# An adaLN + S4D convolution + ReLU MLP kernel: the last doubling ahead of h's shift, kernel products between h's transforms, and two butterfly steps summed on TensorE

## The chip, the cores and the metric

The kernel runs as one program on one core of a Trainium2 chip. The metric is the device time of one execution in microseconds (us), as the median of three runs; smaller is better. Five engines work side by side and meet at semaphores: TensorE (PE, with its weight loads as PEld), VectorE (DVE), ScalarE (ACT), GpSimd (POOL) and SyncE (SP, which here only issues DMAs). Each of them works through its own instructions strictly in the order in which the program lists them.

## The reference

One block of a network on x of 2048 tokens by 576 channels, all in float32. `c` gives six modulation vectors, a layer norm and a long convolution along the tokens are added to x, and then a layer norm and a two-layer ReLU network of width 4608:

```
mod = (silu(c) @ w_mod).reshape(1, 6, 1, 576)      # sa, ca, ga, sb, cb, gb
h = layernorm(x) * (1 + ca) + sa
x = x + ga * conv(h)                                # below
h = layernorm(x) * (1 + cb) + sb
x = x + gb * (relu(h @ w1) @ w2)

def conv(u):                                        # one filter of 2048 taps for each channel
    dt = exp(log_dt);  A = -exp(log_A_real) + 1j * A_imag
    C = (C_real + 1j * C_imag) * dt
    P = exp(A * dt * pos)                           # 576 x 128 states x 2048 positions
    K = 2 * real(sum over states of C * P)
    return irfft(rfft(K, 4096) * rfft(u, 4096))[:2048] + u * D_skip
```

## The kernel before

**Blocks.** The tokens are cut into four blocks of 512, and the filter into four pieces of 512 taps. `Body.conv(s)` does the convolution of block s in the frequency domain, `Body.ffn` the ReLU network of the same block; the convolution of block s+1 is worked off in pieces inside the network of block s (`step`). Only block 0 has nothing to hide behind: what runs before the network of block 0 starts is called the front part here. The change touches the front part alone.

**The front part** makes the first filter piece, transforms it and block 0, multiplies, and transforms back. All of its instructions carry `Kept(...)` or `keep_in_program_order`, so the order in which the Python code emits them is the order on each engine.

- `KGen.first` makes the filter in six groups g of 96 channels. For each group DVE builds `W1` (16 powers, by four doublings in `doubling`; in the fourth, m == 8, DVE makes four products into `T0`/`T1` and POOL adds them), ACT, DVE and POOL build `W2` (32 powers), and TensorE sums `W2` times `W1` over the states into `kps` (`products`, 96 small matmuls for each of two halves u of a group). ACT copies `kps` into `ke` (`rows`), and SP stores `ke` to DRAM (`kd`) once three groups are done. `kt_0` and `kt` are the two channel halves p = 0, 1 of the piece, loaded back from `kd` in transform layout; half 1 needs group 5, the last one. `skip` adds the D_skip term to one row of `kt`.
- The hooks `"first"`, `"late"` and `"rows"` of `conv(0)` are the last group's products of half u = 0, of half u = 1, and then `save` (W1 to DRAM), the copy to `ke` and the store to `kd`.
- `Body.early` is a generator that `first` advances: statistics of x, the normalised `h`, then `h`'s shift, which is eight DVE operations (times `m_ca`, plus `m_sa`).
- A spectrum is made in two stages. `transform` does eight matmuls of 128x288 (four tiles n2 by real and imaginary part c) into `ps_f`, and ACT copies each to `Z`. Then `butterfly` combines the four tiles on DVE in two steps: `butterfly1` (sums and differences of tiles i and i+2, four operations, into `W`) and `butterfly2` (six operations, into `U` or `K`). `transform1` does the first step on TensorE instead: 16 matmuls that accumulate in pairs, the second of a pair with `fcK` or with its negative `fcKn`. Before the change half 1 of the filter takes `transform1`, half 0 takes `transform`.
- `product` multiplies K and U into `Y`, `back` is the inverse's butterfly on DVE into `V`, and `inverse` does the inverse's matmuls into `ps_i`, which DVE adds to x. For half 0 `back` does only the first step and `inverse` the second on TensorE (16 matmuls, some with `gcn`, the negatives of `gc`); for half 1 `back` does both steps and `inverse` 8 matmuls.
- `norm2` follows: statistics, scaling, transposes `ps_t`, then `xh`, `xl`, `xs`, the operands of the network. The first matmul `hps` of `ffn` ends the front part.

A float32 matmul shows in the profile as two records of PE, so eight matmuls of a transform are x16.

**Queues and buffers around it.** POOL issues the saves of the spectra (`Ud` for U, `Rd` for K of block 0); SP issues `kd`, `kt`, the modulation weights `wm_sb`, `wm_cb`, `wm_gb`, the saves of W1, W2 and the network's weights (`r`, with `L1d`/`L2d` the stores of their low halves). Spectra share six buffers (`S`), so a later tile waits until an earlier one has been read and saved. `mod_late` makes three modulation vectors on TensorE (`mps_sb`, `mps_cb`, `mps_gb`). In `ffn`, `hi1`/`hi2` (ACT) and `lo1`/`lo2` (DVE) split a weight tile into a high and a low part.

Of the kernel before, what the change touches and what calls it, by code (L numbers as in the profile page):

```python
# [49 lines left out]
class KGen:  # L50
# [274 lines left out]
    def first(self, setup, mod):  # L325
# [43 lines left out]
        def run(*gens):  # L369
            for x in gens:  # L370
                for _ in x:
                    pass
# [24 lines left out]
        for g in range(NG):  # L397
# [26 lines left out]
            else:  # L424
                run(late, double[3])
            if g + 1 == NG:
                next(early)
            if g > 0:
                rows(g - 1)
            run(*double[4:])  # L430
            if g + 1 < NG:
                save(g)
# [141 lines left out]
class Body:  # L574
# [34 lines left out]
    def early(self, kg):  # L609
# [11 lines left out]
        for i in range(4):  # L621
            yield
            st = sm.tile([P, 2, 6], F32, tag="st", bufs=8, name="st0")
            for p in range(2):
                kept(nc.vector.bn_stats(out=st[:, p], in_=x2[:, i, p * PC : (p + 1) * PC]))
            kept(nc.vector.bn_aggr(out=mv[:, i, 0:2], in_=st))
# [8 lines left out]
        for i in (0, 2, 1, 3):  # L635
            kept(nc.scalar.activation(
                h[:, i], x2[:, i], AF.Identity, scale=mv[:, i, 3:4], bias=mv[:, i, 4:5]
            ))
        yield
        self.kt0 = kg.kt0  # L640
        kept(self.skip(self.kt0, 0, nc.vector))
        for i in (0, 2, 1, 3):
            kept(nc.vector.tensor_tensor(h[:, i], h[:, i], self.m["ca"], op=ALU.mult))
            kept(nc.vector.tensor_tensor(h[:, i], h[:, i], self.m["sa"], op=ALU.add))
# [294 lines left out]
    def conv(self, s):  # L939
# [11 lines left out]
        else:  # L951
            x2, h = self.x2[0], self.h0
            self.fcKn, self.gcn = (
                self.cv.tile([P, 4, P], F32, name=n) for n in ("fcKn", "gcn")
            )
            for t, a in zip((self.fcKn, self.gcn), self.I["neg"]):
                nc.gpsimd.dma_start(out=t, in_=a)
        def kernel_tile(p):
# [13 lines left out]
        def mm_K(p, Z):  # L972
# [3 lines left out]
            src = lambda n2: ktv[:, n2 // 2, :, n2 % 2]  # L976
            if s == 0 and p == 1:
                return self.transform1(src, self.fcK, self.fcKn, Z)
            return self.transform(src, self.fcK, Z, s == 0)

        def spec_U(p, Z):
            U = self.spec(f"U_{s}_{p}")
            yield from self.butterfly(Z, U, -1)
            yield -1
            if s + 1 < NB or p == 1:
                self.save(self.Ud[s][p], U)
            Us.append(U if s == 0 or p == 0 else None)

        def spec_K(p, Z):
            R = self.load(self.Rd[s - 1][p], "R") if s > 0 else None  # L990
            K = self.spec(f"K_{s}_{p}")
            yield from (self.butterfly2 if s == 0 and p == 1 else self.butterfly)(Z, K, -1)
            yield -1
# [50 lines left out]
        def inverse(p, V, tiles=(0, 2, 1, 3)):  # L1044
            g = lambda n2, c: self.gc[:, n2, c, :]
            neg = lambda i: self.gcn[:, i, :]
            for n2 in tiles:
                ps = self.cps.tile([P, 512], F32, tag="cps", bufs=self.nps, name="ps_i")
                if s or p == 1:
                    ops = [(g(n2, c), V[:, n2, c]) for c in range(2)]  # L1050
# [16 lines left out]
        def back(p, Y):  # L1067
            V = self.spec(f"V_{s}_{p}")
            yield from self.butterfly1(Y, V) if s == 0 and p == 0 else self.butterfly(Y, V, 1)
            Vs.append(V)  # L1070
# [4 lines left out]
        if s == 0:  # L1075
            yield from mm_K(0, ZK)
            yield from mm_U(0, ZU)
            Z1 = self.spec("Z")
            yield from mm_U(1, Z1)
            for hook in ("first", "late", "rows"):  # L1080
                yield hook
            kt[1] = kernel_tile(1)
            yield "weights"
            yield "mod"
            yield "mod"
            yield "mod"
            yield "high"
            yield from spec_U(0, ZU)
            yield from spec_U(1, Z1)
            yield from spec_K(0, ZK)  # L1090
            ZK = self.spec("Z")
            yield from mm_K(1, ZK)
            self.save(self.Rd[0][0], Ks[0], Kept(self.tc, nc.gpsimd))
        else:
# [170 lines left out]
    def ffn(self, gens):  # L1265
# [166 lines left out]
        yield  # L1432
        lo1(0)
        lo2(0)
        lo1(1)
        yield
        load_r2(1)
# [200 lines left out]
```

## Time and profile before

| | |
|---|---|
| median of 3 runs | 1322.19 us (1321.43 to 1322.21) |
| the profiled execution, its own time | 1322.81 us |
| its span (first to last instruction) | 1321.0 us |
| mean granted TensorE clock | 0.946 |
| PE busy, share of the span | 1210.7 us, 92% |
| DVE busy, share of the span | 895.0 us, 68% |
| DMA, mean over the span | 262 GB/s |
| first `hps` matmul (end of the front part) | 220.30 us |

All times below are from the span's start. In a timeline a line gives start, length, engine, source line, operation, out<-in, shapes, count, and in brackets the idle time of the engine ahead of it with what ended it. Operations of a helper have the helper's line: L62 is DVE in the filter generator, L68 its POOL, L71 its matmuls, L47 any `Kept` operation, L852 the matmuls of `transform`, L891 and L893 those of `transform1`, L1059 those of `inverse`. In the chain of waits "issue" is time in which an engine waited for nothing that the profile shows.

### The profile page before, as it was taken

How to read it: one execution, taken by the hardware profiler on the slowest of the kernel's cores; microseconds unless marked ns; L12 is line 12 of the kernel's file. 1: busy time of each engine (PE TensorE's matmuls, PEld its weight loads, DVE VectorE, ACT ScalarE, POOL GpSimd, SP SyncE). 2: the span in 40 equal slices, each digit the busy share in tenths (PEclk: the TensorE clock that was granted, in tenths of full speed). 3: DMA queues.
4: the chain of work that ended last, by engine and by line, in shares of the span. 5: the costliest groups of instructions: out<-in, count | busy, mean ns of one | idle time of the engine just before them, and what ended most of it. 6: DMA issues, size and time to landing. Idle time of an engine off the chain costs nothing.

```text
span 1321.0 us, 25994 instructions
## 1 busy us (share of the span) xinstructions
PE 1210.7 (92%) x10720; PEld 959.5 (73%) x10720; DVE 895.0 (68%) x1324; ACT 494.8 (37%) x863; POOL 160.3 (12%) x256
## 2 busy tenths in 40 slices
PE   4666686999999998999999999999999999999998
PEld 2444564677767776787777887887888888888886
DVE  7889988999976999589468994557996222111112
ACT  5787523222223422622243225433323452233231
POOL 1666411011000100110011000100000000000000
PEclk9556787999899999999999999999999999999999
DMA  8757982988778977799889985868996667666662
GB/s 274 269 200 289 322 304 85 349 308 322 286 256 303 345 241 262 261 406 336 279 276 336 360 323 156 294 198 294 343 382 198 172 179 227 202 194 197 195 178 71
DMA packets 118027, 345.85 MB, mean 262 GB/s; under 512 B 17772, under 2 KB 19604, under 8 KB 107156
## 3 DMA queue, kind: packets, MB, share of 16 engines
q1 hardware_dynamic: 101332, 228.14, 51.9%
q0 software_dynamic: 16064, 114.67, 23.0%
q8 instruction: 84, 1.38, 0.4%
q10 hardware_dynamic: 512, 1.38, 0.4%
q14 instruction: 35, 0.29, 0.1%
HBM read 262.73 MB, written 81.40 MB: 261 GB/s over the span
## 4 chain that ended last, share of the span: by engine, by line
PE 75%; DVE 14%; DMA 6%; issue 4%; ACT 1%; POOL 1%; SPq 0%; ACTq 0%; DVEq 0%; POOLq 0%
PE hps L1332 31%; PE acc L1358 30%; PE ps_f L852 5%; PE kps L519 3%; PE kps L71 2%; DMA L1d<-w 2%; PE ph L71 2%; PE ps_i L1059 2%; DVE T L484 1%; DVE W1r L486 1%; DMA x<-in_x_dram 1%; DVE T L62 1%; DMA Ua<-Ud 1%; DVE W L62 1%; DVE w L1302 1%
## 5 line engine op out<-in xcount | busy, mean ns | idle before, releaser
L1332 PE MATMUL hps<-xh,w 128*128 128x512 f32 x1152 | 394.2, 403 | 0.8 <-ACT xh L47 0.8
L1358 PE MATMUL acc<-w,hh 128*128 128x512 f32 x1136 | 362.1, 401 | 4.9 <-ACT hh L1337 3.4
L1338 DVE SCALAR_TENSOR_TENSOR hl<-hps,hh 128x512 fp32r<-128x512 f32 x144 | 99.2, 689 | 306.9 <-ACT hh L1337 306.2
L1332 PEld LDWEIGHTS hps<-xh,w 128*128 128x128 f32 x1152 | 217.8, 190 | 48.3 <-ACT xh L47 1.4
L1358 PEld LDWEIGHTS acc<-w,hh 128*128 128x128 f32 x1136 | 212.5, 188 | 51.3 <-ACT hh L1337 4.3
L1332 PE MATMUL hps<-xl,w 128*128 128x512 f32 x576 | 227.4, 396 | 0.0
L1358 PE MATMUL acc<-w,hl 128*128 128x512 f32 x568 | 221.0, 402 | 1.6 <-DVE hl L1338 1.6
L1337 ACT ACTIVATE hh<-hps 128x512 fp32r<-128x512 f32 x144 | 86.0, 597 | 324.7 <-PE hps L1332 317.5
L1307 ACT ACTIVATE w<-r 128x576 fp32r<-128x576 f32 x141 | 96.7, 686 | 229.0 <-PE acc L1358 221.4
L1332 PEld LDWEIGHTS hps<-xl,w 128*128 128x128 f32 x576 | 109.1, 189 | 22.9
L1358 PEld LDWEIGHTS acc<-w,hl 128*128 128x128 f32 x568 | 106.9, 190 | 25.3 <-DVE hl L1338 3.0
L1297 ACT ACTIVATE w<-r 128x640 fp32r<-128x640 f32 x140 | 102.6, 733 | 40.6 <-DMA L1d<-w 38.1
L1332 PE MATMUL hps<-xs,w 128*128 128x512 f32 x288 | 98.3, 411 | 0.0
L71 PE MATMUL kps<-W,W 128*32 128x16 f32 x2304 | 40.3, 211 | 44.9 <-POOL W L68 28.4
L1038 DVE TENSOR_TENSOR Y<-Y,T 128x1152 f32<-128x1152 f32 x60 | 79.4, 1351 | 0.0
L71 PEld LDWEIGHTS kps<-W,W 128*32 128x32 f32 x2304 | 35.5, 145 | 58.8 <-POOL W L68 31.0
L853 ACT ACTIVATE Z<-ps_f 128x288 f32<-128x288 f32 x120 | 48.9, 409 | 71.9 <-PE ps_f L852 70.1
L519 PEld LDWEIGHTS kps<-W1r,W2r 128*32 128x32 f32 x3456 | 45.1, 113 | 37.8 <-issue 23.1
L519 PE MATMUL kps<-W1r,W2r 128*32 128x48 f32 (+2 forms) x3456 | 52.5, 201 | 14.4 <-issue 8.8
L1332 PEld LDWEIGHTS hps<-xs,w 128*128 128x128 f32 x288 | 53.5, 189 | 11.2
L1358 PE MATMUL acc<-hh,w 128*128 128x512 f32 x142 | 56.7, 399 | 0.0
L1358 PE MATMUL acc<-hl,w 128*128 128x512 f32 x142 | 56.0, 394 | 0.0
(249 smaller groups left out, 1543.5 us busy)
## 6 DMA issues: line engine op xcount, KB each, us to landing
r<-in_w_dram SPq DMA_DIRECT2D x144, 320.0 KB, 5.9
r<-in_w_dram SPq DMA_DIRECT2D x144, 288.0 KB, 3.6
w<-L1d SPq DMA_DIRECT2D x108, 320.0 KB, 3.9
w<-L2d SPq DMA_DIRECT2D x108, 288.0 KB, 2.7
W2r<-W2d POOLq DMA_DIRECT2D x18, 1536.0 KB, 8.8
W2d<-W SPq DMA_DIRECT2D x12, 1536.0 KB, 8.5
Ua<-Ud POOLq DMA_DIRECT2D x15, 1152.0 KB, 9.4
W<-W1d POOLq DMA_DIRECT2D x18, 768.0 KB, 9.4
```

Source lines behind the costliest of these rows:

```text
L62: self.tc.keep_in_program_order(self.nc.vector.tensor_tensor(out, a, b, op=op))
L71: self.tc.keep_in_program_order(self.nc.tensor.matmul(*args, **kw))
L519: nc.tensor.matmul(ps[32 * dd : 32 * dd + 32, q, :], W2[:, r, ch], W1[:, r, ch], start=(r == 0), stop=(r == 1),)
L852: nc.tensor.matmul(o, fc[:, n2, c, :], src(n2), start=True, stop=True)
L853: ev = nc.scalar.activation(Z[:, n2, c], ps[:, :PC], AF.Copy)
L1038: v(y, y, T, op=op or ALU.add)
L1297: copy(g - 1)(w1[g][:, 0], r1[g], AF.Copy)
L1307: copy(g)(w[:, 0:D], r2[g], AF.Copy)
L1332: nc.tensor.matmul(ps, a, x, start=(i == 0), stop=(i == 13))
L1337: nc.scalar.activation(hh, ps, AF.Relu)
L1338: nc.vector.scalar_tensor_tensor(hl, ps, 0.0, hh, op0=ALU.max, op1=ALU.subtract)
L1358: nc.tensor.matmul(acc[i], a, x, start=(f == 0 and seen[i] == 1), stop=(f == NF - 1 and seen[i] == (3 if i < 4 else 2)),)
```

## The change

Six edits, all in the front part.

1. In `first`, the step of `early` with h's shift comes after the last group's fourth doubling instead of before it; `skip` of `kt_0` moves from that step into the one before.
2. Filter half 0 is transformed with `transform1` (16 matmuls instead of 8), so `spec_K(0)` does only `butterfly2`. `fcKn` is loaded by SP early instead of by POOL late.
3. `conv(0)` runs the last group's products of half u = 0 ahead of h's first transform, and those of half u = 1 with the copy and store of `ke` between h's two transforms. Before, all of them came after both.
4. The spectrum of the filter half comes ahead of the two of h on DVE. The saves of U and K (`Ud`, `Rd`) are issued by POOL after `skip` of `kt`.
5. The modulation vector gb is made after the transform of filter half 1 instead of before it.
6. For output half 1, `back` does only the first step (four operations into V, in another order than before), and `inverse` does the second on TensorE. `lo2(0)` and `lo1(1)` of the network's weights move to the next step of `ffn`, behind `norm2`.

```diff
@@ KGen.first
-            if g + 1 == NG:
-                next(early)
             if g > 0:
                 rows(g - 1)
             run(*double[4:])
+            if g + 1 == NG:
+                next(early)
@@ Body.early
         for i in range(4):
             yield
+            if i == 1:
+                self.fcKn = sm.tile([P, 4, P], F32, name="fcKn")
+                nc.sync.dma_start(out=self.fcKn, in_=I["neg"][0])
...
-        yield
         self.kt0 = kg.kt0
         kept(self.skip(self.kt0, 0, nc.vector))
+        yield
         for i in (0, 2, 1, 3):
             kept(nc.vector.tensor_tensor(h[:, i], h[:, i], self.m["ca"], op=ALU.mult))
@@ Body.conv
-            self.fcKn, self.gcn = (
-                self.cv.tile([P, 4, P], F32, name=n) for n in ("fcKn", "gcn")
-            )
-            for t, a in zip((self.fcKn, self.gcn), self.I["neg"]):
-                nc.gpsimd.dma_start(out=t, in_=a)
+            self.gcn = self.cv.tile([P, 4, P], F32, name="gcn")
+            nc.gpsimd.dma_start(out=self.gcn, in_=self.I["neg"][1])
@@ mm_K
-            if s == 0 and p == 1:
+            if s == 0:
                 return self.transform1(src, self.fcK, self.fcKn, Z)
-            return self.transform(src, self.fcK, Z, s == 0)
+            return self.transform(src, self.fcK, Z)
@@ spec_U
-            if s + 1 < NB or p == 1:
+            if s and (s + 1 < NB or p == 1):
                 self.save(self.Ud[s][p], U)
@@ spec_K
-            yield from (self.butterfly2 if s == 0 and p == 1 else self.butterfly)(Z, K, -1)
+            yield from (self.butterfly if s else self.butterfly2)(Z, K, -1)
@@ inverse
-                if s or p == 1:
+                if s:
                     ops = [(g(n2, c), V[:, n2, c]) for c in range(2)]
@@ back
-            yield from self.butterfly1(Y, V) if s == 0 and p == 0 else self.butterfly(Y, V, 1)
+            if s:
+                yield from self.butterfly(Y, V, 1)
+            else:
+                for i, op in ((0, ALU.add), (1, ALU.add), (0, ALU.subtract), (1, ALU.subtract)):
+                    v(V[:, 2 * i + (op == ALU.subtract)], Y[:, i], Y[:, i + 2], op=op)
+                yield -1
@@ conv, block 0
             yield from mm_K(0, ZK)
+            yield "first"
             yield from mm_U(0, ZU)
+            yield "late"
+            yield "rows"
             Z1 = self.spec("Z")
             yield from mm_U(1, Z1)
-            for hook in ("first", "late", "rows"):
-                yield hook
             kt[1] = kernel_tile(1)
             yield "weights"
             yield "mod"
             yield "mod"
-            yield "mod"
             yield "high"
+            yield from spec_K(0, ZK)
             yield from spec_U(0, ZU)
             yield from spec_U(1, Z1)
-            yield from spec_K(0, ZK)
             ZK = self.spec("Z")
             yield from mm_K(1, ZK)
-            self.save(self.Rd[0][0], Ks[0], Kept(self.tc, nc.gpsimd))
+            for dst, t in ((self.Ud[0][0], Us[0]), (self.Rd[0][0], Ks[0]), (self.Ud[0][1], Us[1])):
+                self.save(dst, t, Kept(self.tc, nc.gpsimd))
+            yield "mod"
@@ ffn
         lo1(0)
+        yield
+        lo1(1)
         lo2(0)
-        lo1(1)
-        yield
```

Where the instructions stand is shown at three places. First TensorE and VectorE around h's shift. `kps_2248` (after: `kps_2250`) holds the last group's products, `W_5` is its W1, `W_10` and `W_11` are its W2 of the halves u = 0 and 1, `fcU` is h's transform matrix, `mps_sb` the first late modulation vector. TensorE before:

```order
L71 MATMUL kps_1942<-W_4_1712,W_9_1706 32x16 x96
L852 MATMUL ps_f<-kt_1943,fcK 128x288 x8
L852 MATMUL ps_f<-h_2099,fcU 128x288 x16
L71 MATMUL kps_2248<-W_5_2048,W_10_2041 32x16 x96
L71 MATMUL kps_2248<-W_5_2048,W_11_2042 32x16 x96
L733 MATMUL mps_sb<-wm_sb,cb 32x128 x20
```

TensorE after (the 16 matmuls of filter half 0 stand in single rows; the last two are shown):

```order
L894 MATMUL ps_f<-kt_1945,fcK 128x288
L896 MATMUL ps_f<-kt_1945,fcKn 128x288
L71 MATMUL kps_2250<-W_5_2050,W_10_2043 32x16 x96
L855 MATMUL ps_f<-h_2101,fcU 128x288 x8
L71 MATMUL kps_2250<-W_5_2050,W_11_2044 32x16 x96
L855 MATMUL ps_f<-h_2101,fcU 128x288 x8
L736 MATMUL mps_sb<-wm_sb,cb 32x128 x20
```

The products now stand ahead of and between h's two transforms. VectorE before, from the last of h's shift:

```order
L644 TENSOR_TENSOR h_2099<-h_2099,m_sa 128x576
L62 TENSOR_TENSOR T_2236<-W_5_2048,Zp_2082 128x768
L62 TENSOR_TENSOR T_2237<-W_5_2048,Zp_2082 128x768
L62 TENSOR_TENSOR T_2242<-W_5_2048,Zp_2082 128x768
L62 TENSOR_TENSOR T_2243<-W_5_2048,Zp_2082 128x768
L47 TENSOR_TENSOR W<-Z 128x576 x4
L47 TENSOR_TENSOR U_0_2671<-W 128x576 x2
L47 TENSOR_TENSOR U_0_2671<-W 128x288 x4
```

VectorE after, from the last product of the doubling:

```order
L62 TENSOR_TENSOR T_2235<-W_5_2050,Zp_2084 128x768
L646 TENSOR_TENSOR h_2101<-h_2101,m_ca 128x576
L647 TENSOR_TENSOR h_2101<-h_2101,m_sa 128x576
...
L47 TENSOR_TENSOR K_0_2649<-Z 128x576 x2
L47 TENSOR_TENSOR K_0_2649<-Z 128x288 x4
L47 TENSOR_TENSOR W<-Z 128x576 x4
L47 TENSOR_TENSOR U_0_2656<-W 128x576 x2
```

The doubling's four products moved ahead of the shift, and K_0 comes straight from Z, ahead of U_0, with no W of its own. Second, the saves on POOL before:

```order
L843 DMA Ud_0_101<-U_0_2671 128x2304
L843 DMA Ud_1_102<-U_1_2684 128x2304
L47 TENSOR_TENSOR kt<-kt,m_gb 1x4x72
L47 DMA Rd_0_109<-K_0_2697 128x2304
L843 DMA Rd_1_110<-K_1_2762 128x2304
```

and after:

```order
L47 TENSOR_TENSOR kt<-kt,m_gb 1x4x72
L47 DMA Ud_0_101<-U_0_2656 128x2304
L47 DMA Rd_0_109<-K_0_2649 128x2304
L47 DMA Ud_1_102<-U_1_2668 128x2304
L846 DMA Rd_1_110<-K_1_2762 128x2304
```

Both saves of U moved behind `skip` of `kt` (the TENSOR_TENSOR). Third, the network's first weights on SP before:

```order
L1281 DMA r_2944<-in_w_dram 128x576
L1277 DMA r_2942<-in_w_dram 128x640
L1449 DMA L1d_127<-w_2664 128x640
L1449 DMA L2d_163<-w_2668 128x576
L1449 DMA L1d_128<-w_2665 128x640
L1281 DMA r_3005<-in_w_dram 128x576
```

and after:

```order
L1456 DMA L1d_127<-w_2642 128x640
L1284 DMA r_2946<-in_w_dram 128x640
L1288 DMA r_2948<-in_w_dram 128x576
L1456 DMA L1d_128<-w_2643 128x640
L1456 DMA L2d_163<-w_2646 128x576
L1288 DMA r_3009<-in_w_dram 128x576
```

Two loads (`r_2946`, `r_2948`) now need the buffers that `lo1(1)` and `lo2(0)` free, and two stores need their results; all four stand behind those two splits. Behind this point every engine's order is the same as before.

## The prediction

> **What bounds the kernel now.** I read the chain of waits of 158 to 227 us first, then DVE's and PE's own timelines there, then the granted clock and the DMA share in short windows. The chain of the front part:
>
> ```profile
> 161.00 5.68 issue
> 166.68 1.95 PE kps L71 x111
> 168.63 2.05 issue
> 170.68 1.31 PE kps L71 x73
> 172.07 0.50 ACT ke L59
> 173.11 2.55 DMA kd<-ke
> 175.71 5.39 DMA kt<-kd
> 181.27 1.31 POOL kt L47
> 182.58 8.80 DMA Rd<-K
> 191.47 0.23 DVE K L47
> ```
>
> The end of the front part hangs on the last group's products (kps): they end at 171.99, go out to DRAM and back as kt, which takes until POOL's skip is done at 182.6, and then K_1, the spectrum of filter half 1, waits for the save of K_0, issued behind that skip. 7.7 us of it is "issue": PE stands still inside the products. DVE's side of the same time:
>
> ```profile
> 143.74 0.44 DVE L1263 TENSOR_TENSOR kt<-kt,m_gb 1x288 f32<-1x288 f32 x1
> 144.11 0.74 DVE L643 TENSOR_TENSOR h<-h,m_ca 128x576 f32<-128x576 f32 x1
> 149.95 3.54 DVE L62 TENSOR_TENSOR T<-W,Zp 128x768 f32<-128x768 f32 x4
> 166.42 2.75 DVE L47 TENSOR_TENSOR W<-Z 128x576 f32<-128x576 f32 x4
> 169.10 2.89 DVE L47 TENSOR_TENSOR K<-W 128x576 f32<-128x576 f32 x6
> 171.91 2.62 DVE L47 TENSOR_TENSOR Y<-K,U 128x1152 f32<-128x1152 f32 x2
> 179.88 3.36 DVE L47 TENSOR_TENSOR V<-Y 128x576 f32<-128x576 f32 x4
> 183.16 0.81 DVE L47 TENSOR_TENSOR w<-r,w 128x640 fp32r<-128x640 f32 x1
> 184.38 1.56 DVE L47 TENSOR_TENSOR w<-r,w 128x64 fp32r<-128x64 f32 x3 [0.40 <-ACT w L47]
> 191.47 2.90 DVE L47 TENSOR_TENSOR K<-Z 128x576 f32<-128x576 f32 x6 [5.53 <-DMA Rd<-K]
> 203.60 2.76 DVE L47 TENSOR_TENSOR W<-Y 128x576 f32<-128x576 f32 x4
> 206.28 2.90 DVE L47 TENSOR_TENSOR V<-W 128x576 f32<-128x576 f32 x6
> 214.77 0.45 DVE L47 TENSOR_TENSOR x<-ps_i,x 128x288 f32<-128x288 f32 x1
> 226.85 0.69 DVE L1338 SCALAR_TENSOR_TENSOR hl<-hps,hh 128x512 fp32r<-128x512 f32 x1 [1.48 <-ACT hh L1337]
> ```
>
> DVE is busy almost throughout, is done with half 0 at 183.2, fills 2.4 us with the split of weights, and stands still for 5.53 us ahead of K_1. So the most that the earlier products alone can give is about 8 us (191.47 less 183.2); more needs DVE's own chain to shorten. PE:
>
> ```profile
> 137.02 1.95 PE L71 MATMUL kps<-W,W 128*32 128x16 f32 x128 [2.71 <-issue]
> 140.75 0.66 PE L71 MATMUL kps<-W,W 128*32 128x16 f32 x31 [1.78 <-issue]
> 144.39 7.09 PE L852 MATMUL ps_f<-kt,fcK 128*128 128x288 f32 x16 [2.98 <-issue]
> 151.32 7.92 PE L852 MATMUL ps_f<-h,fcU 128*128 128x288 f32 x32
> 159.18 1.82 PE L71 MATMUL kps<-W,W 128*32 128x16 f32 x174
> 207.17 6.43 PE L1059 MATMUL ps_i<-V,gc 128*128 128x288 f32 x16 [8.71 <-DVE V L47]
> ```
>
> Two things stand in these rows. The stops come every 128 records of PE (128 between the stops of 2.71 and 1.78, 128 again between those of 5.68 and 2.05), and the queue named "instruction" moved 16.4 KB a packet: PE waits for the next block of its own instructions. And a transform's record costs 0.44 us in one row (7.09/16) and 0.25 in the next (7.92/32): the clock.
>
> ```profile
> 148.00:150.00 2.00, 2.00 (x6) 1.43 (x5) 1.97 (x4) 0.88 (x3) 0.00 (x0) 0.50 0.82 311
> 150.00:152.00 2.00, 2.00 (x9) 1.54 (x8) 2.00 (x4) 1.23 (x3) 0.15 (x1) 0.90 1.01 382
> 164.00:166.00 2.00, 0.00 (x0) 0.00 (x0) 2.00 (x5) 0.00 (x0) 0.00 (x0) 0.52 1.07 428
> 210.00:212.00 2.00, 2.00 (x6) 1.36 (x6) 1.57 (x5) 0.29 (x1) 0.00 (x0) 0.54 0.00 0
> 230.00:240.00 10.00, 10.00 (x46) 8.13 (x45) 10.00 (x11) 3.13 (x6) 0.53 (x1) 1.00 1.01 402
> ```
>
> (Busy time of PE, PEld, DVE, ACT, POOL, then the granted clock, the DMA share, GB/s.) The clock rises to full 6 us after the transforms start at 144.39, falls to half 3 us after PE stopped at 161.00, and rises 4.7 us after ps_i starts at 207.17. The DMA engines are full at 150 to 166 and again from 230. Four more rows, of DMA issues, of the queues (packets, MB, share) and of the chain, price that:
>
> ```profile
> fcKn<-in_neg_dram POOLq DMA_DIRECT2D x1, 256.0 KB, 7.7
> W1d<-W SPq DMA_DIRECT2D x1, 768.0 KB, 15.3
> q8 instruction: 84, 1.38, 0.4%
> 240.39 9.66 DMA L1d<-w
> ```
>
> A small load issued at 142.3 behind 3 MB of saves lands after 7.7 us, a save issued at 153.8 after 15.3.
>
> **The change part by part.** Times of the changed kernel are in the clock of this execution.
>
> *Doubling ahead of h's shift, skip ahead of both.* DVE's sum is unchanged: 3.54 us of products come 5.8 us sooner (the shift's 144.11 to 149.95), so behind the skip they run from 144.2 (143.74 + 0.44) to 147.7, POOL's additions are done by about 150.5, the shift runs from 147.7 to 153.5. h's first transform has to wait for the shift's last quarter; it waits for PE anyway (next).
>
> *Half 0 by 16 matmuls.* PE is free of the fourth group at 141.41 (140.75 + 0.66) and kt is ready, so it starts there instead of at 144.39. 32 records, the first 5 us at 0.44 (the two rises took 4.7 and 6), the rest at 0.25: 10 us, done at 151.5 instead of 151.3. DVE saves one W<-Z, 2.75 us.
>
> *Products between the transforms.* The first half (192 records, about 2 us at the full clock) runs 151.5 to 153.8. Counted in blocks of 128 from the stops above, a new block begins at its very end and another 128 records on, early in the second half. Each of the four stops seen is 1.8 to 5.7 us; hidden it costs 0. For the first I take 3.5 us (the four rows average 3.1, and DMA is full here), for the second 1 us, because the transform's 16 records ahead of it (3.9 us) cover most of it. So h's first transform runs 157.3 to 161.2, the products end at 164.3 instead of 172.0, h's second transform ends at 168.2, its last copy at 168.8. From the products' end through DRAM to POOL's skip it is 10.6 us now (171.99 to 182.6), so kt is ready at about 175, and the transform of half 1 starts there; the two modulation vectors still ahead of it on PE end there too. With its 32 records of 0.25 and the last copy it takes 8.5 us: K_1's input is there at 183.6.
>
> *DVE's order.* K_0 2.9 us from 153.5 ends at 156.4; U_0 waits for its copies and ends near 166; U_1 waits for the copy at 168.8, and half a W (1.35) and U (2.89) on it is done at 173.0, 1.1 us later than the row Y starts now (171.91). Products and V are 11.3 us (171.91 to 183.2), one split 0.8: DVE reaches K_1 at 185.3. That is later than its inputs, so **DVE starts K_1 at 185.3 instead of 191.47: -6.2 us**. The saves moved behind skip cost nothing if they land by then: K_1 takes the buffer of U_0, whose save is the first behind skip, like K_0's now: issued at 175.1, with 8.8 us landing at 183.9. K_0's own save is second and needed 2.9 us later. POOL itself is idle behind them. `fcKn` moved to SP costs 0.7 us of DMA long before; its cover is the 80 us until it is read.
>
> *gb's vector behind half 1* puts its matmuls (2.2 us) ahead of the first inverse on PE. The four inverse tiles were ready 3 us ahead of DVE's additions; they are now about 1 us ahead. Cost 0 (to 0.4 if PE is cold).
>
> *Output half 2.* DVE saves 2.3 us (2.76 + 2.90 less 3.36), PE does 32 records instead of 16. PE ends the first inverse about 11 us after K_1 starts (its 32 records, behind gb) and gets the first V it needs at 15.7 (Y's end at 12.1, the first two operations, the first dispatch): 4.5 us idle, more than the 3 us after which the clock fell twice; so it starts at half clock, with a first tile of 8 records in 3.5 us, and rises after 4.7 us. It starts 1.6 us after Y ends instead of 3.6 (203.57 to 207.17); 10.7 records at 0.44 and 21.3 at 0.25 end 11.5 us after Y. The last addition to x stood 11.2 us after Y (214.77 less 203.57). **+0.4 us**; at the full clock throughout it would be -1.6.
>
> *The splits behind norm2.* 1.56 us go into the gap of 1.48 us ahead of hl, and the second hps waits for the first of them: **+0.2 us**. What they free is late too: two loads and two stores, 1.2 MB, move from a time when DMA had room into 226 to 240, where it is full at 402 GB/s: 3.0 us of transfers. DVE is busy for 10.00 of 10 us there, so part hides behind DVE; but the chain goes through a store of 9.66 us at 240.39. Between 0 and +3.0 I take **+1.2 us**.
>
> Sum: -6.2 + 0.4 + 0.2 + 1.2 = **-4.4 us**. On the profiled execution (1322.81, of which the span is 1321.0) that is 1318.4; the median lies 0.6 lower, so **1317.8 us**. Behind the front part the orders are the same and PE is 9 to 10 tenths busy, so I carry the gain to the end undiminished.
>
> [...]
>
> **Rivals.**
>
> - *Stops hidden.* With no stop ahead of or inside the second products, h's transforms end at 157.7 and 163.2 and DVE runs K_0, U_0, U_1 without a gap to 167.7, then to 179.8. The store of ke then waits behind W1's saves (by the traffic issued, less U's, about 164), kt is back near 173 to 175, K_1 starts at 182: -9.5, with the other terms 1314.5. For it: the transform ahead covers 3.9 us. Against it: four stops in the last five blocks of products. Chance 0.13.
> - *Stops long: slower.* The stop ahead of h's first transform is one mechanism that reverses the sign, since DVE has no other work for it. If that fetch waits like the small load of 7.7 us and then 2.4 us for itself, PE restarts at 163 to 164 with the clock at half, the transform takes 7 us, the next block is late too, and the second transform ends at 178: K_1 at 195.1, +3.6, in all 1327.6. It is even when the second transform ends at 172.6, and a loss that can be told when it ends at 175.2. For it: DMA is full at 152, and the longest stop of 5.68 us fell into the same traffic. Against it: two saves of 1.15 MB leave this stretch. Chance 0.09.
> - *The gain is spent.* K_1 comes 4 to 6 us sooner, but the 1.2 MB delay the store in the chain by the whole 3.0 us, or U_1 comes at 171 to 172.6: -2.6 to 0, near 1320.8. Chance 0.23.
> - *The change does not shorten the chain at all*, because K_1 still waits for a save: it waits for U_0's, and with 15.3 us instead of 8.8 it starts at 190.4. The other terms then make it 1322.9. Chance 0.05, since SP's saves of W1 are out by then.
>
> **How the numbers follow.** The forecast's own case (-2.6 to -7) has 0.50. Less than 0.2% (2.6 us) is about what a measurement of this kernel cannot tell from no change. Faster: 0.50 + 0.13 = 0.63; same: 0.23 + 0.05 = 0.28; slower 0.09. The range 1313.5 to 1322.5 takes in the hidden stops below and the spent gain above, and leaves out the long stops and half of the last rival. The forecast's own range is 1315.2 to 1319.6.
>
> **What would show it.** Right: kps ends near 164 and kt is skipped near 175; PE has a gap of 2 to 5 us between the two halves of the products, ahead of h's first transform; no DMA stands ahead of K_1 on DVE, which starts it at 184 to 187; ps_i of half 1 takes about 10 us and starts at half clock; hps starts near 216. Wrong: U_1 after 175, a save as the releaser of K_1, or a first hps 6 us earlier with an end that is not.

## The result: slower by 12.9 us

| | before | changed |
|---|---|---|
| median | 1321.81 us (4 runs, 1320.87 to 1322.21) | 1334.69 us (4 runs, 1333.65 to 1339.71) |
| ratio | | 1.0096 (1.0076 to 1.0116) |
| profiled execution, its own time | 1322.81 us | 1334.19 us |
| its span | 1321.0 us | 1332.4 us |
| mean granted clock | 0.946 | 0.947 |
| first `hps` matmul | 220.30 us | 222.22 us |
| first `hl` | 226.85 us | 228.67 us |
| fourth `hl` | 256.62 us | 264.36 us |
| tenth `hl` | 312.69 us | 324.18 us |
| last `hl` | 1309.41 us | 1319.22 us |

`hl` is the DVE operation that follows each `hps`, 144 times in the kernel. Nothing in the order of the network's instructions differs, so the n-th `hl` of two executions can be set side by side. The changed kernel is 1.8 us late at the first, 7.7 at the fourth, 11.5 at the tenth and 9.8 at the last (the 1.6 us up to the span's 11.4 lie in the landing of the last store). So the gain forecast for the front part is not there, and most of the loss falls within 100 us behind it. Slow executions (four in the series below, of 1340 to 6597 us) are left out of all figures.

**The front part.** The chain of waits of the changed kernel, to be laid beside the one of before:

```profile
152.42 2.00 PE kps L71 x145
154.43 5.49 issue
159.92 0.19 PE kps L71
160.10 7.07 PE ps_f L855 x16
167.18 1.16 PE kps L71 x87
168.33 0.40 issue
168.73 1.02 PE kps L71 x62
...
170.81 2.54 DMA kd<-ke
...
173.43 5.75 DMA kt<-kd
...
179.34 3.66 POOL kt L47
```

The save of K_0 is gone from it, as forecast. But the stop ahead of h's first transform took 5.49 us, the transform behind it 7.07 us for 16 records (0.44 us each, the price of the half clock: the granted clock is 0.50 from 156 to 166 us), and POOL's skip 3.66 us instead of 1.31. The stop fits the fetch of instructions that the prediction names: the one packet of queue q8 (instruction) in it starts at 157.5 us, 3 us after PE stopped, and PE restarts 2.4 us later. For each of the eight stops inside the products between 134 and 171 us (four in each profile, before and changed) such a packet starts 2.2 to 2.9 us before PE restarts. DVE's timeline shows who waited:

```profile
146.21 3.54 DVE L62 TENSOR_TENSOR T<-W,Zp 128x768 f32<-128x768 f32 x4
149.66 1.02 DVE L646 TENSOR_TENSOR h<-h,m_ca 128x576 f32<-128x576 f32 x1
150.72 1.44 DVE L647 TENSOR_TENSOR h<-h,m_sa 128x576 f32<-128x576 f32 x1
152.08 1.56 DVE L646 TENSOR_TENSOR h<-h,m_ca 128x576 f32<-128x576 f32 x1
...
157.28 2.89 DVE L47 TENSOR_TENSOR K<-Z 128x576 f32<-128x576 f32 x6
164.72 1.43 DVE L47 TENSOR_TENSOR W<-Z 128x576 f32<-128x576 f32 x2 [4.54 <-ACT Z L856]
167.66 1.43 DVE L47 TENSOR_TENSOR W<-Z 128x576 f32<-128x576 f32 x2 [1.51 <-ACT Z L856]
...
178.45 2.62 DVE L47 TENSOR_TENSOR Y<-K,U 128x1152 f32<-128x1152 f32 x2
...
192.26 2.90 DVE L47 TENSOR_TENSOR K<-Z 128x576 f32<-128x576 f32 x6 [1.86 <-ACT Z L897]
```

DVE gets to Y at 178.45 instead of 171.91 and to K_1 at 192.26 instead of 191.47. What K_1 waited less for its input, DVE waited earlier, ahead of W and U.

Behind K_1 DVE loses another 1.7 us: from K_1's start to the end of the last Y it is 13.8 us instead of 12.1. gb's matmuls (`mps_gb`) now stand ahead of the first inverse, so DVE's four additions to x wait 1.3 us in sum for its tiles. The first inverse and the first addition, before and changed:

```profile
190.54 3.07 PE L1059 MATMUL ps_i<-V,gc 128*128 128x288 f32 x12
195.56 0.46 DVE L47 TENSOR_TENSOR x<-ps_i,x 128x288 f32<-128x288 f32 x1
```

```profile
192.68 2.22 PE L736 MATMUL mps_gb<-wm_gb,cb 128*32 128x128 f32 x50
194.84 3.18 PE L1059 MATMUL ps_i<-V,gc 128*128 128x288 f32 x12
197.08 0.46 DVE L47 TENSOR_TENSOR x<-ps_i,x 128x288 f32<-128x288 f32 x1 [0.65 <-PE ps_i L1059]
```

The same 13.8 us stand in all nine profiles with this place of gb in which K_1 waits for its transform (those of all three runs with the second half last, below, are among them); in the five in which DVE comes to K_1 later than that, and in the six with gb's old place, it is 12.1. No run moved gb back alone.

**The network's start.** ACT's timeline, first of before, then of the changed kernel:

```profile
231.12 0.73 ACT L1297 ACTIVATE w<-r 128x640 fp32r<-128x640 f32 x1
232.59 0.69 ACT L1307 ACTIVATE w<-r 128x576 fp32r<-128x576 f32 x1 [0.75 <-PE acc L1358]
235.77 0.60 ACT L1337 ACTIVATE hh<-hps 128x512 fp32r<-128x512 f32 x1 [2.49 <-DVE W1r L490]
```

```profile
242.26 0.74 ACT L1304 ACTIVATE w<-r 128x640 fp32r<-128x640 f32 x1 [9.11 <-DMA L1d<-w]
245.74 0.68 ACT L1314 ACTIVATE w<-r 128x576 fp32r<-128x576 f32 x1 [2.74 <-DMA L2d<-w]
246.33 0.58 ACT L1344 ACTIVATE hh<-hps 128x512 fp32r<-128x512 f32 x1
```

The two copies write into weight buffers (three in rotation) whose low halves are being stored. Before, those stores were issued before 190 us; now they come out of the splits behind norm2. In both timelines ACT takes the two copies and the third `hh` in the order of the program, so the `hh` stands behind the copies: 246.33 instead of 235.77, and PE waits for it (5.85 us). The chain of waits goes through the second store:

```profile
230.09 15.55 DMA L2d<-w
```

15.55 us for 288 KB, because POOL's loads for the next filter piece are in flight. The queues from 230 to 245 us (packets, MB, share of the engines), before and changed:

```profile
q0 software_dynamic: 704, 4.60, 76.0%
q1 hardware_dynamic: 641, 1.40, 24.2%
```

```profile
q0 software_dynamic: 646, 4.60, 75.3%
q1 hardware_dynamic: 611, 1.33, 23.5%
```

All 16 engines are full in both, at 401 and 396 GB/s, but SP's queue (q1) moves only 1.33 to 1.40 MB of the 6 in 15 us: 90 KB per us. At that rate 1.2 MB more in the queue are not 3 us of transfers but 13 (an estimate). The two queues get about the same number of packets, and SP's are 2.2 KB while POOL's are 6.5 to 7.1 KB.

### The profile page after: what moved, and what is told of

Its sections match the earlier page's. It is cut to its first block, busy times and chain, and to the rows that moved or that the text cites. A ratio compares the mean times of both kernels' runs of the same rounds, so it can differ in the third digit from the quotient of the medians.

```text
span 1332.4 us, 26041 instructions
## 1 busy us (share of the span) xinstructions
PE 1222.4 (92%) x10752; PEld 966.1 (73%) x10752; DVE 891.3 (67%) x1314; ACT 495.1 (37%) x863; POOL 163.0 (12%) x255
## 4 chain that ended last, share of the span: by engine, by line
PE 71%; DVE 12%; DMA 7%; issue 5%; ACT 1%; POOL 1%; SPq 1%; ACTq 0%; DVEq 0%; POOLq 0%
PE hps L1339 28%; PE acc L1365 28%; PE ps_f L855 3%; DMA L1d<-w 3%; PE ps_i L1059 3%; PE kps L71 3%; PE ph L71 2%; PE kps L519 2%; DVE T L484 1%; DVE W1r L486 1%; DMA L2d<-w 1%; DVE W1r L488 1%; DMA kd<-ker 1%; DVE W1r L490 1%; POOL W L68 1%
## 5 line engine op out<-in xcount | busy, mean ns | idle before, releaser
L856 ACT ACTIVATE Z<-ps_f 128x288 f32<-128x288 f32 x112 | 45.9, 410 | 76.0 <-PE ps_f L855 74.7
L1339 PEld LDWEIGHTS hps<-xs,w 128*128 128x128 f32 x288 | 53.5, 189 | 11.5 <-DVE w L47 0.4
## 6 DMA issues: line engine op xcount, KB each, us to landing
Ua<-Ud POOLq DMA_DIRECT2D x15, 1152.0 KB, 10.2
```

The costliest lines, as they stand in the source:

```text
L856: ev = nc.scalar.activation(Z[:, n2, c], ps[:, :PC], AF.Copy)
L1339: nc.tensor.matmul(ps, a, x, start=(i == 0), stop=(i == 13))
```

## The experiments

In the later series single executions of the kernel before scatter from 1316 to 1333 us, so each kernel ran 6 to 12 times, beside 23 to 35 runs of before on the same chip. "Over before" below is the ratio less one, times 1322 us, with its 95% interval. The differences of the medians deviate from it by up to 2.7 us.

### The splits

*Both splits back*, twice:

```diff
         lo1(0)
-        yield
-        lo1(1)
         lo2(0)
+        lo1(1)
+        yield
```

> The changed kernel with the two splits of weights back ahead of the spectrum of filter half 1. Theory A (the loss lies in the DMA queues: 1.2 MB of loads and stores that the splits free come in SP's queue at 229 us, while POOL's burst of 5.6 MB holds the engines, and SP's queue moves only 110 KB per us there, so that a store lands 15.6 us after its issue and the copy of weights behind it, and then hh and PE, wait): the lateness of 1.8 us with which the first hps starts stays, the 9 us behind it go: 1323 to 1326 us. Theory B (the network loses because it starts later and in another phase, wherever the splits stand): 1333 to 1336 us.

> The changed kernel with the splits back and nothing else, a second time (7.3 us over before in the first series). If the place of the borders costs what the first series say (7.3 against 0 for two kernels with the borders realigned): 5 to 9 us over before. If that was the scatter of executions, as the repetition of the shifted kernel before suggests (4.5, then 0.5): 0 to 4 us over before, the front part's 2 us being what is left.

Measured: 7.3 us over before (4.1 to 10.6) and 4.1 (1.7 to 6.6). ACT's two copies no longer wait and the fourth `hl` is as late as the first:

```profile
234.02 0.73 ACT L1304 ACTIVATE w<-r 128x640 fp32r<-128x640 f32 x1
235.49 0.69 ACT L1314 ACTIVATE w<-r 128x576 fp32r<-128x576 f32 x1 [0.75 <-PE acc L1365]
```

*The splits alone*: the kernel before with only this part of the change.

> The kernel before, with nothing changed but that the two splits of weights stand behind norm2. Theory A: the front part loses nothing or gains up to 1.5 us, the network loses 6 to 10 us: 1327 to 1332 us, with a store of about 15 us in the chain at 230 us. Theory B: 1320 to 1323 us.

6.7 us over before (4.0 to 9.5), with the same store in its chain, `227.37 16.50 DMA L2d<-w`.

*One split late* (`lo2(0)` back, `lo1(1)` late), and *the stores in a queue of their own*:

```diff
-                for dst, src in late:
-                    nc.sync.dma_start(out=dst, in_=src.bitcast(F32))
+                for i, (dst, src) in enumerate(late):
+                    e = Kept(self.tc, nc.scalar) if g == 0 and i else nc.sync
+                    e.dma_start(out=dst, in_=src.bitcast(F32))
```

> The changed kernel with only the split of w2 (group 0) back, the split of w1 (group 1) stays behind norm2. The store that the copy waited for in the changed kernel, L2d of group 0, is then issued before 195 us; half of the 1.2 MB stay in the burst. Theory A1 (the wait for just this store is the loss): 1324 to 1327 us. Theory A2 (every byte in SP's queue at that time costs, whichever store is last): half the loss stays, 1328 to 1331 us. Theory B: 1333 to 1336 us.

> The changed kernel with the splits where it has them, but the two stores behind them (L1d of group 1, L2d of group 0) issued by ACT, in a queue of their own, ahead of hh. The bytes in the burst are the same. Theory A2 in the form that the share of SP's queue is short (110 KB per us): the stores take a share of their own and land some 5 us sooner, 1326 to 1330 us. If it is the engines' total rate that is short (400 KB per us, all full), nothing is gained: 1333 to 1336 us.

6.7 us (3.2 to 10.2) and 8.3 (4.2 to 12.3): too wide to tell A1 from A2 by the time. The traces tell more, with one profile each. How much later than the first the fourth `hl` is, compared with before:

| splits | profiles | us over before |
|---|---|---|
| both late | changed, changed again, changed with borders realigned (below), splits alone | 5.9, 5.4, 5.2, 6.2 |
| one late | 1 | 2.8 |
| both late, stores in ACT's queue | 1 | 2.8 |
| ahead of K_1 | all 13 others of this study | -1.1 to 0.9 |

So theory A holds: the splits' place costs 5 to 6 us there, by itself as well as within the change. Half the bytes in SP's queue cost about half (A2 rather than A1). The stores in ACT's queue save less than their row says: on ACT they stand ahead of the first `hh` and wait for the splits, so the first `hl` itself comes 7.6 us after the first `hps` instead of 6.3 to 6.6. Counted from the first `hps`, that profile is 3.8 us over before at the fourth `hl`, against 5.1 to 6.1 with both late in SP's queue.

### The borders of PE's instruction blocks

With the splits back 4 to 7 us are still missing. The change gives PE 32 records more (10752 instead of 10720), which shifts the border of each block of 128 behind them (128 records lie between the stops of 2.71 and 1.78 us before, and 128 between those of 3.07 and 2.16 us in the changed kernel). To move borders and nothing else, I put in tiny matmuls on constants whose results are overwritten.

```diff
+                for i in range(48 if s == 0 and p == 1 and n2 == 0 else 0):
+                    r, c = 32 * (i % 4), 16 * (i // 4)
+                    nc.tensor.matmul(
+                        ps[r : r + 32, c : c + 16], self.ident[:, 0:32], self.ident[:, 0:16],
+                        start=True, stop=True,
+                    )
```

(Between the two inverses, in `inverse`, 16 of them for a shift of 32; the early variant writes into `ps[g]` ahead of the fourth group's products.) A first series missed, since each of them gives two records, so the shifts were twice those meant, and the ones ahead of norm2's transposes, all written to one place, put 4.3 us on the path (last addition to x to first `hps`: 9.4 us instead of 5.1):

> The changed kernel with the splits back (6.9 us over before), and 96 tiny matmuls on constants more on TensorE ahead of the products of the fourth group, where PE idles for 4.9 us. They change nothing but the place of the borders between PE's blocks of 128 matmuls: behind them the borders lie as in the kernel before (32 records of the change and 96 make 128), and the border at the end of the first half of the last products (a stop of 4.2 to 5.5 us ahead of h's first transform in four profiles) moves 96 records ahead, so that the half transform of 10 us runs while the next block is fetched. Theory C (what is left of the loss, 6.9 us, is where the borders of PE's blocks fall): stop gone, K_1 some 4 us sooner, 1319 to 1325 us, 0 to 3 us over before at most. Theory D (it is not the blocks): 5 to 8 us over before, as with the splits back alone.

> The changed kernel with the splits back and the 96 tiny matmuls just ahead of norm2's transposes instead: the front part keeps its borders and its stop of 4 to 5 us, the network has the borders of the kernel before. Theory C1 (the network's part of the loss is its shifted borders): 2 to 4 us over before. Theory C2 (the borders matter in the front part alone) and D: 5 to 8 us over before.

> The kernel before with 32 tiny matmuls on constants more, ahead of norm2's transposes, so that the network's block borders lie as in the changed kernel; nothing else is changed. Theory C1: 3 to 6 us over before. C2 and D: 0 to 1 us over before.

> The changed kernel once more, on the same chip as the three others: 11 to 15 us over before by every theory; it gives the scatter of its executions.

They took 9.5 us (6.9 to 12.3), 5.2 (2.8 to 7.5) and 5.8 (3.4 to 8.1) over before; less the 4.3 us, the last two are 0.9 and 1.5. The changed kernel again: 12.6 (9.4 to 15.9). In the first of the three the stop ahead of h's transform is gone, but others of 4.63 us (inside the fourth group) and 4.79 us (behind h's first transform) take its place, Y comes at 184.59 and the first `hps` at 226.66. That is not the work of moved borders alone: its 192 records, to one place as well, take 10.4 us, and counted from PE's first product behind 107 us the fourth group's products start 6.3 us later than in the changed kernel.

The second series, with the shifts right:

> The kernel before with 16 tiny matmuls on constants more, between the first and the second inverse, where PE idles 8.7 us. Each gives two records in the trace (the last series had twice the shift meant, and its matmuls ahead of norm2's transposes cost 4.3 us, since they wrote one place over and over), so these 32 records shift the borders of PE's blocks in the network by 32, as the changed kernel does; nothing else is changed. Theory C1 (that shift costs the network 4 to 6 us, as five profiles with it against five without suggest): 3 to 7 us over before. Theory C2 and D (the borders in the network don't matter): 0 to 1 us over before.

> The changed kernel with the splits back (7.3 us over before) and 48 such tiny matmuls between its two inverses, where PE idles 4.1 us: 96 records, so that with the 32 of the change the borders lie in the network as in the kernel before. The front part keeps its borders. Theory C1: 0 to 3 us over before. C2 and D: 5 to 9 us over before.

> The changed kernel with the splits back and the 48 tiny matmuls ahead of the products of the fourth group, in PE's gap of 4.9 us: the network's borders as before, and in the front part the border that fell at the end of the first half of the last products (stop of 4.2 to 5.5 us ahead of h's first transform) falls ahead of the transform of half 0 instead, where a stop costs up to 3 us. Theory C1 with the front's stops counted: from 3 us less than before to 2 us over. If only the network's borders count: 0 to 3 over. D: 5 to 9 over.

> The changed kernel as it is, splits behind norm2, with the 48 tiny matmuls between the two inverses. Theories A and C1 together: what is left of 12.7 us is the splits' share, 5 to 8 us over before, and the trace shows the loss at the fourth hl (some 5 to 6 us) and little behind it. D: 11 to 14 us over before.

Before, shifted by 32: 4.5 us over before (1.1 to 7.9). Splits back, borders as before: -0.9 (-4.0 to 2.0), and -0.3 (-3.0 to 2.6) with the matmuls early (by the medians 1.6 and 1.7). Changed with borders as before: 8.7 (5.9 to 11.4). That spoke for C1, so I repeated its most direct test, beside another shift:

> The kernel before with the network's borders shifted by 32 records, a second time: theory C1: 3 to 7 us over before as in the first series (4.5), and where the profile is of a slow execution, a stop inside the products at 285 to 292 us and POOL's load of W2 behind it 13 to 16 us after the one ahead instead of 10 to 11. If the first series was chance: 0 to 1 us over.

> The kernel before with the borders shifted by 96 records (48 tiny matmuls between the inverses). C1 in the form that only some places of the borders cost (the border inside the products at 285 to 292 us): 0 to 2 us over before, as the two earlier profiles with that shift had 0.3 us more in the network. If any shift costs: 3 to 7 us over before.

0.5 us (-2.4 to 3.6) and 0.3 (-3.4 to 3.8). The shift of 32 does not reliably cost in the kernel before. What the profile shows is how a border can cost. First the kernel before with the shift of 32, in its second series: PE's products, POOL's loads of W2, the chain of waits:

```profile
285.61 0.42 PE L519 MATMUL kps<-W1r,W2r 128*32 128x16 f32 x10 [3.23 <-issue]
```

```profile
276.36 0.53 POOL L47 DMA_DIRECT2D W2r<-W2d  x1 [6.41 <-PE kps L519]
293.07 0.53 POOL L47 DMA_DIRECT2D W2r<-W2d  x1 [15.13 <-PE kps L519]
```

```profile
294.85 12.04 DMA L1d<-w
```

Then the changed kernel with the splits back, in its second series, POOL and the chain:

```profile
282.22 0.53 POOL L47 DMA_DIRECT2D W2r<-W2d  x1 [7.87 <-PE kps L519]
292.33 0.53 POOL L47 DMA_DIRECT2D W2r<-W2d  x1 [8.54 <-PE kps L519]
```

```profile
299.25 7.61 DMA L1d<-w
```

With the stop inside the products POOL's next load of W2 comes later (16.7 us after the last one instead of 10.1); its burst then starts just ahead of the store in the chain, which takes 12 us instead of 7.6. In the 20 profiles there are six with a stop of over 2 us in these products, between 284 and 297 us: there the step from the ninth to the tenth `hl` is 2.0 to 3.75 us longer than before; in the other 14 it is 1.4 shorter to 1.3 longer. With the shift of 32 the stop is in four of eight profiles (both of the changed kernel among them, 3.22 and 2.64 us), with all other places in two of twelve. That may mean that a place of the border makes the stop likelier; eight and twelve profiles are too few to show it.

### The front part

*The second half of the last products behind both of h's transforms*, splits back, borders as before (late, then early matmuls, and the early one again):

```diff
             yield from mm_U(0, ZU)
-            yield "late"
-            yield "rows"
             Z1 = self.spec("Z")
             yield from mm_U(1, Z1)
+            yield "late"
+            yield "rows"
```

> The changed kernel with the splits back, the borders in the network as before (48 tiny matmuls between the inverses), and the second half of the last products moved from between h's two transforms to behind both: nothing else on any engine moves but ACT's copies. Theory F1 (the front part's gain was lost because PE's stops inside the last products, 5 to 6 us in sum, lie ahead of h's transforms, so that DVE gets U_1 4 to 6 us later than forecast): the first product Y comes at 171 to 174 us instead of 178 to 179, K_1 at 186 to 189 instead of 190 to 191, in all 1 to 4 us under before. Theory F2 (DVE is late for other reasons, the slower shift of h and the cold clock): Y after 176, 0 to 2 us over before.

> The same with the 48 tiny matmuls ahead of the fourth group's products instead, so that the borders of the front part are shifted too. F1: as the run before within 1.5 us, since the stops now lie where PE's work is not waited for: 1 to 4 us under before. F2: 0 to 2 us over before.

> The kernel with the second half of the products behind h's transforms and the tiny matmuls early, a second time: it was 2.9 us under before with an interval from 5.7 under to none. By theory F1 the front part is 2 to 4 us shorter and the network as before: 1 to 4 us under before again.

-0.4 us (-3.0 to 2.2), -2.9 (-5.7 to 0.0) and -0.8 (-3.6 to 1.9). In the profile of the last one, PE and DVE:

```profile
153.89 8.03 PE L862 MATMUL ps_f<-h,fcU 128*128 128x288 f32 x32
161.85 1.39 PE L71 MATMUL kps<-W,W 128*32 128x16 f32 x125
165.53 0.81 PE L71 MATMUL kps<-W,W 128*32 128x16 f32 x66 [2.29 <-issue]
```

```profile
168.17 2.62 DVE L47 TENSOR_TENSOR Y<-K,U 128x1152 f32<-128x1152 f32 x2
185.91 2.90 DVE L47 TENSOR_TENSOR K<-Z 128x576 f32<-128x576 f32 x6 [4.33 <-ACT Z L904]
```

With the early matmuls (both profiles) h's transforms run at full clock (32 records in 8.03 us in each, 0.25 us a record) straight behind the shift, and the stop lies behind them, where DVE has work: Y at 168.2 and 169.5, against 177.8 with the same borders and the second half between the transforms. With the late matmuls a stop of 3.17 us is still ahead of the transforms, and Y comes at 174.2 against 179.2. (In all ten profiles of the changed order, without the run of 192 records, Y comes at 174.1 to 180.0; in the six of the order before at 169.0 to 171.9.) From PE's first product behind 107 us to the first `hps` the profiles give:

| order | profiles | us |
|---|---|---|
| before | 5 | 107.0 to 110.4, mean 108.7 |
| changed, splits late or back | 9 | 109.3 to 113.9, mean 110.9 |
| changed, second half last | 3 | 105.4 to 107.6, mean 106.7 |

(The three of the first border series are left out, since their matmuls lie in the path.)

So theory F1 holds in the traces: the front part is 2.2 us longer with the change, not 5.6 shorter, and moving the second half behind h's transforms takes 4.2 us off it. That it is then 2.0 us shorter than before is not shown: in the one series on one chip that has both, the order before took 107.0 and 107.3 us and the second half last 107.3 and 107.6. In the time of the kernel this shows as 0.4 to 2.9 us less than before, within what can be told; two runs of the best version do not prove a gain over before. Over the changed kernel it is a gain of more than 10 us, with the splits back and the borders moved as well.

## Why the prediction was wrong

Forecast were 1317.8 us (1313.5 to 1322.5); measured are 1334.7. Two terms of the sum failed: the -6.2 us at K_1 (steps 3 and 4; the stop was priced too short) and the +1.2 us for 1.2 MB (step 7; priced by the wrong rate). A third, gb's vector, was put at nothing and cost 1.7 us (step 5). In the profiled execution the first `hps` is 1.9 us late: +0.8 at K_1, +1.7 for gb, -0.5 for output half 2. The fourth `hl` is 5.8 us later still, the last 2.1 more, and the landing of the last store 1.6.

1. *Doubling, skip and shift.* Right in kind, 3.8 us off: the shift ended at 157.3 instead of 153.5. 1.1 us is the clock, which the earlier products of before were granted and these were not (a window of before, then of the changed kernel; behind POOL's busy time stands the granted clock, 1.00 and 0.50):

```profile
98.00:100.00 2.00, 1.93 (x52) 1.33 (x52) 1.90 (x6) 1.62 (x4) 2.00 (x3) 1.00 0.09 33
```

```profile
98.00:100.00 2.00, 2.00 (x36) 1.50 (x36) 1.90 (x6) 1.41 (x2) 2.00 (x3) 0.50 0.05 22
```

   Three operations of the shift took 1.02, 1.44 and 1.56 us instead of 0.75 (1.8 us in sum), while POOL's additions ran beside them (148.1 to 153.0): I moved the additions into the shift and priced both as if alone. And DVE's skip, moved to where POOL is at work on W, took 1.33 us instead of 0.44: the last 0.9.
2. *Half 0 by 16 matmuls.* Right: done at 152.3, forecast 151.5 with 1.1 us of clock to add.
3. *Stops.* For the first 3.5 us were taken, a little over the mean of four rows (3.1); it was 5.49, and the clock fell behind it, so that 16 records took 7.1 us instead of 3.9. The products ended at 169.7 instead of 164.3. This is the mechanism of the rival "stops long", which had 0.09; the profile offered its 5.68 us row in just this traffic. A step behind it, POOL's skip took 3.66 us and `kt` was ready at 183.0, not 175.
4. *K_1.* Forecast 185.3 (its own terms, 173.0, 11.3 and 0.8, give 185.1), in fact 192.3 (191.1 without the clock's 1.1): the term of -6.2 us was -0.3 in this execution without the clock and +0.8 with it, and over all profiles of this order the front part is longer by 2.2.
5. *Saves, fcKn.* Right: no save stands ahead of K_1. *gb's vector.* Forecast 0 to 0.4 us, measured 1.7. The forecast had DVE reach K_1 1.7 us after its transform was done, so that the first inverse kept ahead; in fact K_1 waited for the transform, and gb's 2.2 us on PE pushed the inverse behind DVE's additions.
6. *Output half 2.* Forecast +0.4 us; the last addition to x starts 10.7 us after Y ends instead of 11.2, so -0.5. The half clock at its start (granted 0.54 from 207 to 208 us and 0.50 from 208 to 210) and the length of 9.7 us came as described.
7. *1.2 MB of loads and stores.* This is the step that cost most behind the front part: forecast +1.2 with bounds 0 and +3.0, measured +5.2 to +6.2 at the fourth `hl`. I priced the bytes at the engines' total rate of 402 GB/s and let DVE's work hide them. But the bytes stand in one queue with a quarter of that rate (90 KB per us), and I did not follow the new wait through its engine: store, weight buffer, ACT's copy, the `hh` queued behind it, PE. The upper bound came from the total rate too, so the range could not hold it.
8. *"I carry the gain to the end undiminished."* Wrong as well: from the first `hl` to the last it is -2.0 and +4.9 us against before in two executions of one kernel (before, shifted by 32), and the changed kernel's two profiles lie 2.1 and 8.2 us over before behind the fourth `hl`. Where POOL's bursts meet SP's stores is 2 to 3.75 us of that at the one place traced; the rest was not traced.

What stays open: how much of the 12.9 us belongs to the borders of PE's blocks on the average. The splits are 5 to 6 us by the traces, and by time 5.4 and 9.6 (the changed kernel, 12.7, against 7.3 with the splits back in the first series; 8.7 against -0.9 with the borders of before in both). Against the second run with the splits back, 4.1, it is 8.6. The front part is 2.2. The other 4 to 5 us went when the borders were realigned (from 7.3 and 4.1 to -0.9 and -0.3), but by the medians from 6.9 and 3.0 to 1.6 and 1.7 only, the intervals of 4.1 and the last two overlap, and the same shift alone gave 4.5 us once and 0.5 once.

## What to carry to other kernels

Before an operation is moved into a stretch where DMA is full, price what it frees by the rate of its own queue there, and follow the buffer to the next writer and to everything queued behind that writer. Dense bursts of small matmuls brought their instruction stops with them here (0.40 to 5.68 us each): put them where nobody waits for PE, behind the work that others wait for. A term put at nothing because one engine comes later than another has to be looked at again when the order of the two turns. And a gain of a few us ahead of a stage in which two queues collide can only be told from the scatter by many runs.

## What the runs showed that was not expected

- In the full DMA stretch the two queues got about the same number of packets (704 and 641, 646 and 611), so the one with 2.2 KB packets got a quarter of the bytes. The two stores issued from ACT's queue got 249 packets of their own beside 676 and 674, and the loss at the fourth `hl`, counted from the first `hps`, was 3.8 us in that profile instead of 5.1 to 6.1.
- Three of DVE's operations with two inputs took 1.02, 1.44 and 1.55 us instead of 0.75 beside POOL's additions, in all 14 profiles of the changed order alike. POOL's skip of the same 288 elements took 3.65 to 3.80 us in the six profiles in which it starts 0.7 to 0.9 us behind DVE's first product of Y, and 0.78 to 1.97 us in the other 14.
- 48 tiny matmuls to one place in PSUM (96 records) took 3.21 us, 33 ns a record; products to different places ran at 11 ns (192 records in 2.14 us), both at granted clock 1.00.
- Four instruction stops stand within 35 us of the last products (2.71, 1.78, 5.68 and 2.05 us before; 3.07, 2.16, 5.49 and 0.40 in the changed kernel). Moving the borders moves them and does not remove them: with the early matmuls and the changed order one of 0.94 and one of 5.07 us lay behind h's first transform, instead of 5.49 ahead of it.
